# Four small marker loads between wq's second half and K in a one-core decode block

## The chip, the cores and the metric

The kernel runs on one core of a Trainium2 chip. The time is device microseconds of one execution; the kernel before took 137.87 us (median of three runs, 137.82 to 137.88). The profile is one further execution, and its times are counted from the start of its span.

## The reference

One decode step (one new token for each of 4 sequences) of an attention block and a gated MLP:

```
q   = layernorm(x) @ wq                       x: 4 x 1024, wq: 1024 x 4096
s   = q . K^T / sqrt(128)                     32 query heads, 4 KV heads, the last 2048 positions
o   = softmax(s) . V
h   = x + o @ wo                              wo: 4096 x 1024
n   = layernorm(h)
out = h + (silu(n @ w1) * (n @ w3)) @ w2      w1, w3: 1024 x 3584, w2: 3584 x 1024
```

All in bfloat16. With 4 rows of activations there is little arithmetic for each byte: the weights and the caches, 55.6 MB, are each read once.

## The kernel before

All big loads go through the sync queue (SP) into one buffer in SBUF, `ring`, of 160 KB in each partition. They are written out by hand in the list `plan`: wq's first half (4 of 8 blocks of rows), two "side" loads, wq's second half, K in four loads (two plan entries), V in four, wo, w1, w3 and w2 in four pieces of 17, 7, 3 and 1 rows. `load_next(n)` issues the next n entries. Seven are issued at the start (up to the first half of V), and the rest at fixed places in the program, once the ring's place is free: the second half of V after wq's first four blocks, wo after half of K, w1 after half of the V products, w3 in the wo product, and so on.

The side loads deserve a word. wq's second half leaves out the last 512 columns of its last block of rows (`load_tail`, line 126). Those come by `load_side` (line 120) as 20 and as 12 rows of four pieces of 1 KB, into tiles of the pool `ktpool`, and the q product takes them with eight matmuls of its own (line 273). `ktpool` has four buffers that are used in turn: the two side tiles take the first two, then the 16 transposed K tiles `kT` and four tiles `z` of the softmax follow.

Two small loads of x for the residual (`x_q`, line 169, 4 KB each) also go through SP, after the first seven entries. The first x (`x_sb`, line 158) and the output use the queue of ScalarE (ACT).

The framework gives each load on SP or ACT one of eight completion semaphores in turn. A load whose semaphore is still used by an earlier load makes its queue wait until that load has landed. So the position of a load in the program decides which earlier landing it waits for. In the kernel before, the fourth K load waits for wq's first half, the two first V loads for an x load and a side load, and the x_q loads for the other side load and for wq's second half.

The computation follows the loads: layernorm of x and the q product (line 263); for each of 16 pieces of K transposes on TensorE (line 319), copies by VectorE and ScalarE (lines 323 and 325) and scores (line 304); softmax; the V product (line 382); wo (line 411); the second layernorm; gate and up products (line 459); the down product (line 492), whose last 11 rows go to two accumulators that are cast to the result (lines 513 and 514) and stored.

Of the kernel before, what the change touches and what calls it, by code (L numbers as in the profile page):

```python
# [10 lines left out]
P = 128  # L11
# [3 lines left out]
BF16 = mybir.dt.bfloat16  # L15
# [4 lines left out]
def kernel(  # L20
# [13 lines left out]
    nc = tc.nc  # L34
# [23 lines left out]
    ktpool = ctx.enter_context(tc.tile_pool(name="ktpool", bufs=4))  # L58
# [6 lines left out]
    JG = 4  # L65
    QD = P // JG
# [56 lines left out]
    def load_tail(at, src, n, r0, m):  # L123
# [5 lines left out]
    plan = [  # L129
        ("wq", load_rows, (0, wq_v, N_Q, 0, 4)),  # L130
        ("side", load_side, SETS[0]),
        ("side", load_side, SETS[1]),
        ("wq", load_tail, (32 * KIB, wq_v, N_Q, 4, 4)),
        ("k", load_kv, (64 * KIB, A_k_cache, 0)),
        ("k", load_kv, (96 * KIB, A_k_cache, 2)),
        ("v", load_kv, (128 * KIB, A_v_cache, 0)),
        ("v", load_kv, (0, A_v_cache, 2)),
# [5 lines left out]
        ("w2", load_rows, (104 * KIB, w2_v, D, 24, 3)),  # L143
        ("w2", load_rows, (110 * KIB, w2_v, D, 27, 1)),
    ]
    loaded = {}
    cursor = [0]

    def load_next(n=1):
        for _ in range(n):  # L150
            if cursor[0] < len(plan):
                kind, f, args = plan[cursor[0]]
                loaded.setdefault(kind, []).extend(f(*args))
                cursor[0] += 1

    x_sb = act.tile([B, D], BF16)
    for c in range(2):
        nc.scalar.dma_start(out=x_sb[:, c * 512 : (c + 1) * 512], in_=x_flat[:, c * 512 : (c + 1) * 512])
    load_next(7)

    ident = const.tile([P, P], BF16)
    make_identity(nc, ident[:])
# [5 lines left out]
    for c in range(2):  # L168
        nc.sync.dma_start(
            out=x_q[c * 2 * QD : (c + 1) * 2 * QD : RS, :],  # L170
            in_=x_flat.rearrange("b (j c) -> j b c", j=JG)[2 * c : 2 * c + 2],
# [7 lines left out]
    for c in range(2):  # L179
# [8 lines left out]
        out=xn[:], in0=x_sb[:], scalar1=mv[:, 0:1], scalar2=rstd[:, 0:1],  # L188
# [14 lines left out]
    for r0, ne, ns in SETS:  # L203
# [3 lines left out]
            out=xs[:, len(sl) : len(sl) + ns, : ne * 4].rearrange("b l (i s) -> b l i s", s=4),  # L207
            in_=v[:, KC - 1, :, :, :],
        )
        for l in range(ns):  # L210
            nc.tensor.transpose(
                out=ts_ps[: ne * 4, len(sl), :], in_=xs[:, len(sl), : ne * 4], identity=ident[:B, :B]
# [4 lines left out]
    for _, ne, ns in SETS:  # L217
# [14 lines left out]
        out=perm[:].rearrange("p (h dq) -> p h dq", dq=JG),  # L232
        in_=ident[:].rearrange("p (dq h) -> p h dq", dq=JG),
# [12 lines left out]
    for j in range(2, JG):  # L246
        nc.vector.tensor_tensor(
            out=same[:, 0, :], in0=same[:, 0, :], in1=ident[:, j * QD : (j + 1) * QD], op=ALU.add
# [6 lines left out]
    for kc in range(KC):  # L255
        wq_t = loaded["wq"][kc]
        for hf in range(CQ // 512):
            for g in range(JG):
                c0 = g * CQ + hf * 512
                n = min(512, N_Q - CE - c0) if kc == KC - 1 else 512  # L260
# [23 lines left out]
    for r in range(REP):  # L284
        nc.tensor.transpose(out=qt_ps[:, r, :], in_=q_sb[:, r * Dh : (r + 1) * Dh], identity=ident[:])
    nc.vector.tensor_copy(
        out=qz[:, :, : Hkv * QD].rearrange("p b (g z) -> p b g z", g=Hkv)[:, :, :, :REP],
        in_=qt_ps[:].rearrange("p r (g x) -> p x g r", g=Hkv)[:, :B, :, :],
# [24 lines left out]
    for u, (b, n) in enumerate(units):  # L313
        k_v = loaded["k"][b]
        kT = ktpool.tile([P, NJ, P], BF16, tag="kT")
        for t in range(NJ // TB):
            kt_ps = psA.tile([P, TB, P], BF16, tag=f"kt{nt % 4}")
            for jj in range(TB):
                nc.tensor.transpose(  # L319
                    out=kt_ps[:, jj, :], in_=k_v[:, n * NJ + t * TB + jj, :], identity=ident[:]  # L320
# [21 lines left out]
        out=Pm[:], in_=scores_ps[:], func=ACT.Exp, bias=nmax[:], scale=1.0, accum_out=rsum[:]  # L342
# [6 lines left out]
    for c in range(NSB):  # L349
# [4 lines left out]
        for g in range(Hkv):  # L354
            if g % 2 == 0:
                nc.vector.tensor_scalar(  # L356
                    out=z[:, :, g, :], in0=pt_ps[:], scalar1=mask[:, g : g + 1], scalar2=None, op0=ALU.mult
# [10 lines left out]
        out=Dm[:], in0=ident[:].rearrange("p (g b r) -> p b g r", g=Hkv, b=B),  # L368
# [40 lines left out]
    for i in range(IO):  # L409
# [34 lines left out]
        out=hn[:], in0=h1[:], scalar1=tot[:, 0:1], scalar2=rstd2[:, 0:1],  # L444
# [5 lines left out]
        out=hnT[:].rearrange("p k x -> p (k x)"), in_=hn[:].rearrange("q (c k) -> q k c", k=KC)  # L450
# [3 lines left out]
    def gate_up(kind, out_ps):  # L454
# [27 lines left out]
        out=hgT[:].rearrange("p i x -> p (i x)"),  # L482
        in_=hg[:].rearrange("q s c -> q (s c)").rearrange("q (c i) -> q i c", i=IF),
# [62 lines left out]
```

## Time and profile before

| | |
|---|---|
| Time, median of 3 runs | 137.87 us (137.82 to 137.88) |
| Span of the profiled execution | 136.0 us; the page gives no total for that execution |
| Median less that span | 1.87 us |
| PE, DVE, ACT busy | 72.3, 43.9, 31.0 us |
| DMA packets, bytes, mean rate | 2650, 55.75 MB, 410 GB/s |
| of them on SP's queue | 2604 packets, 95.6% of the 16 DMA rings' time |
| wq's first half landed, second half landed | 12.9 us, 23.6 us |
| w1 issued | 76.27 us |
| last wait for a load on the chain | to 130.22 us |

The span goes from the first to the last instruction. "Busy" counts an engine's own instructions, not waiting. The DMA share is the mean busy share of the core's 16 DMA engines, called rings here: each load is cut over several of them, and each ring works its packets off in the order in which they were queued. Beside the page there is a record of every packet (queue, start, length, bytes); a completion is a packet of 4 bytes.

### The profile page before, as it was taken

To read this page: it belongs to the slowest core of one execution; us is meant where nothing else is said; L and a number is where in the kernel's file an instruction comes from. 1 tells how busy PE (TensorE), PEld (TensorE's weight loads), DVE (VectorE), ACT (ScalarE), POOL (GpSimd) and SP (SyncE) were. 2 spreads that over 40 slices of the span, in tenths; PEclk is the share of its full clock that TensorE was granted. 3 is DMA by queue.
4 is the path that set the end of the run, shared out by engine and by line. 5 is a ranking of instruction groups with operands and counts; after the bars stand their busy time and mean duration, and the time that the engine had idled before them with its cause. 6 is when DMAs were issued, how large, how long until landed. Compare 5 with 4: busy or idle time off the path is not lost.

```text
span 136.0 us, 2436 instructions
## 1 busy us (share of the span) xinstructions
PE 72.3 (53%) x1096; PEld 46.1 (34%) x1096; DVE 43.9 (32%) x79; ACT 31.0 (23%) x36; POOL 1.7 (1%) x8
## 2 busy tenths in 40 slices
PE   0004920979898989810525916791097000970981
PEld 0002300268374756500014905570043000430870
DVE  5055000043344444470994001206200596026010
ACT  3000000015555555609294300000001400000000
POOL 5000000000000000000000000000000000000000
PEclk9999975557999999985555555568556855568568
DMA  5999999999999999999989999989989899999970
GB/s 155 464 463 406 412 420 414 429 424 439 424 439 424 424 443 426 410 552 453 463 347 463 463 410 405 477 354 494 439 371 494 371 472 401 399 420 407 424 298 5
DMA packets 2650, 55.75 MB, mean 410 GB/s; under 512 B 296, under 2 KB 464, under 8 KB 720
## 3 DMA queue, kind: packets, MB, share of 16 engines
q1 hardware_dynamic: 2604, 55.58, 95.6%
q8 instruction: 8, 0.13, 0.3%
q10 hardware_dynamic: 36, 0.02, 0.0%
q14 instruction: 2, 0.02, 0.0%
HBM read 55.59 MB, written 0.01 MB: 409 GB/s over the span
## 4 chain that ended last, share of the span: by engine, by line
DMA 54%; PE 25%; ACT 11%; DVE 5%; SPq 2%; issue 1%; ACTq 0%
DMA ring<-in_B_w_dram 38%; DMA ring<-in_A_wq_dram 15%; PE kt_ps L319 11%; ACT kT L325 5%; PE scores_ps L304 5%; ACT z L360 3%; PE q_ps L263 3%; DVE rmax L336 2%; ACT Pm L341 2%; PE OT_ps L382 2%; DVE pT L350 1%; SPq L120 1%; PE g_ps L459 1%; DVE z L356 1%; ACT L341 1%
## 5 line engine op out<-in xcount | busy, mean ns | idle before, releaser
L325 ACT COPY kT<-kt_ps 128x1024 bf16<-128x1024 bf16 x16 | 15.9, 1013 | 13.4 <-PE kt_ps L319 13.4
L319 PE MATMUL kt_ps<-ident,ring 128*128 128x128 bf16 x256 | 18.0, 232 | 0.0
L319 PEld LDWEIGHTS <-ring 128*128 128x128 bf16 x256 | 16.0, 105 | 4.9 <-issue 4.9
L323 DVE COPY kT<-kt_ps 128x1024 bf16<-128x1024 bf16 x16 | 11.1, 692 | 16.5 <-PE kt_ps L319 16.5
L459 PEld LDWEIGHTS <-hnT 128*32 128x32 bf16 x128 | 5.5, 143 | 21.8 <-issue 19.2
L382 PE MATMUL OT_ps<-z,ring 128*128 128x32 bf16 x256 | 7.5, 188 | 8.5 <-ACT z L360 5.0
L459 PE MATMUL u_ps<-ring,hnT 128*32 128x448 bf16 x64 | 6.0, 563 | 11.0 <-DMA ring<-in_B_w_dram 11.0
L304 PE MATMUL scores_ps<-kT,qz 128*32 128x512 bf16 x64 | 9.9, 609 | 2.9 <-ACT kT L325 2.9
L263 PE MATMUL q_ps<-ring,xnT 128*4 128x512 bf16 x63 | 6.7, 595 | 7.8 <-DMA ring<-in_A_wq_dram 7.8
L382 PEld LDWEIGHTS <-ring 128*128 128x128 bf16 x256 | 7.4, 104 | 9.2 <-issue 9.2
L459 PE MATMUL g_ps<-ring,hnT 128*32 128x448 bf16 x64 | 5.9, 558 | 4.9 <-DMA ring<-in_B_w_dram 4.9
L492 PEld LDWEIGHTS <-hgT 128*32 128x32 bf16 x156 | 4.9, 134 | 6.2 <-issue 5.7
L411 PE MATMUL y_ps<-ring,o 128*32 128x256 bf16 x128 | 5.9, 371 | 0.8 <-DVE o L398 0.8
L514 ACT CAST res<-yb_ps 128x128 bf16<-128x128 f32 x1 | 0.3, 266 | 26.1 <-PE yb_ps L492 26.1
L492 PE MATMUL y_ps<-ring,hgT 128*32 128x256 bf16 x68 | 3.8, 419 | 4.4 <-DMA ring<-in_B_w_dram 4.4
L360 ACT ACTIVATE z<-pt_ps,mask 128x512 bf16<-128x512 f32 x8 | 5.3, 687 | 3.5 <-DVE z L356 3.5
L352 PE MATMUL pt_ps<-pT,perm 128*128 128x512 bf16 x4 | 2.4, 607 | 6.8 <-DVE pT L350 6.8
L263 PEld LDWEIGHTS <-xnT 128*4 128x4 bf16 x63 | 2.0, 115 | 11.7 <-issue 11.6
L194 PE MATMUL tp_ps<-ident,xn 4*128 4x4 bf16 x8 | 0.7, 200 | 10.0 <-DVE xn L187 10.0
L356 DVE TENSOR_SCALAR z<-pt_ps,mask 128x512 bf16<-128x512 f32 x8 | 5.5, 741 | 1.2 <-ACT z L360 0.8
L473 DVE RECIPROCAL eg<-eg 128x896 f32<-128x896 f32 x1 | 5.8, 5753 | 0.0
L411 PEld LDWEIGHTS <-o 128*32 128x32 bf16 x128 | 4.4, 131 | 3.1 <-DVE o L398 1.9
(85 smaller groups left out, 50.1 us busy)
## 6 DMA issues: line engine op xcount, KB each, us to landing
ring<-in_B_w_dram SPq DMA_DIRECT2D x2, 7168.0 KB, 22.5
ring<-in_A_k_cache_dram SPq DMA_DIRECT2D x4, 2048.0 KB, 27.6
ring<-in_A_v_cache_dram SPq DMA_DIRECT2D x4, 2048.0 KB, 29.2
ring<-in_B_w_dram SPq DMA_DIRECT2D x1, 4352.0 KB
ring<-in_A_wq_dram SPq DMA_DIRECT2D x1, 4096.0 KB, 12.2
ring<-in_A_wq_dram SPq DMA_DIRECT2D x1, 3968.0 KB
ring<-in_B_w_dram SPq DMA_DIRECT2D x1, 1792.0 KB
ring<-in_B_w_dram SPq DMA_DIRECT2D x1, 768.0 KB
```

What stands on the lines that cost most here:

```text
L263: nc.tensor.matmul(q_ps[QD * g : QD * g + B, hf * 512 : hf * 512 + n], lhsT=xnT[:, kc, :], rhs=wq_t[:, c0 : c0 + n], start=(kc == 0), stop ...
L304: nc.tensor.matmul(scores_ps[QD * g : QD * (g + 1), n * 512 : (n + 1) * 512], lhsT=qz_v[:, z0 : z0 + QD], rhs=kT_v[:, g, :, :], start=(b = ...
L319: nc.tensor.transpose(out=kt_ps[:, jj, :], in_=k_v[:, n * NJ + t * TB + jj, :], identity=ident[:])
L323: nc.vector.tensor_copy(out=kT[:, t * TB : (t + 1) * TB, :], in_=kt_ps[:])
L325: nc.scalar.copy(out=kT[:, t * TB : (t + 1) * TB, :], in_=kt_ps[:])
L356: nc.vector.tensor_scalar(out=z[:, :, g, :], in0=pt_ps[:], scalar1=mask[:, g : g + 1], scalar2=None, op0=ALU.mult)
L360: nc.scalar.mul(out=z[:, :, g, :], in_=pt_ps[:], mul=mask[:, g : g + 1])
L382: nc.tensor.matmul(OT_ps[:, b, :], lhsT=loaded["v"][b][:, j, :], rhs=PTz[j // NJ][:, (j % NJ) * B + b, :, :], start=(j == 0), stop=(j == J ...
L411: nc.tensor.matmul(y_ps[QD * j : QD * (j + 1), :], lhsT=o4[:, i, :, :].rearrange("p b s -> p (b s)"), rhs=loaded["wo"][i][:, j * CG : (j + ...
L459: nc.tensor.matmul(out_ps[QD * j : QD * (j + 1), hf, :HF], lhsT=hnT[:, k, :], rhs=loaded[kind][k][:, c0 : c0 + HF], start=(k == 0), stop=( ...
L473: nc.vector.reciprocal(out=eg[:], in_=eg[:])
L492: nc.tensor.matmul(out_ps[QD * j : QD * (j + 1), :n], lhsT=hgT[:, i, :], rhs=loaded["w2"][i][:, j * CG + c0 : j * CG + c0 + n], **kw,)
```

## The change

A new plan entry is put between wq's second half and the first K entry, so that eight entries are issued at the start. It takes one more tile of `ktpool` and loads into it four small rectangles of wo: 8 rows of 256 bytes, 10 of 320, 12 of 384 and 14 of 448, 16,128 bytes in all. Nothing reads the tile. No other operation is changed, but all later loads move on by four in the round of completion semaphores, and the `kT` tiles by one in the round of buffers: the fourth `kT` tile now follows the marks' tile.

```diff
+    MARKS = (8, 10, 12, 14)
+
+    def load_marks():
+
+        m = ktpool.tile([P, JG * QD * 16], BF16, tag="kT")
+        at = 0
+        for k in MARKS:
+            n = 16 * k
+            nc.sync.dma_start(out=m[:k, at : at + n], in_=A_wo[k * 128 : k * 128 + k, :n])
+            at += n
+        return []
+
+    plan.insert(4, ("marks", load_marks, ()))
...
-    load_next(7)
+    load_next(8)
```

## The prediction

> **What bounds the kernel now.** I read the page's slices first, then the stage table, the SP queue's own timeline with its list of waits, and the chain at the end.
>
> The page of the kernel before: span, DMA slices, and the SP queue's loads.
>
> ```profile
> span 136.0 us, 2436 instructions
> ...
> DMA  5999999999999999999989999989989899999970
> ...
> q1 hardware_dynamic: 2604, 55.58, 95.6%
> ```
>
> From the third slice almost to the end the 16 DMA rings are full, nearly all of it q1, the queue that SP fills. The stage table (columns: stage, its length, busy time of PE, PEld, DVE, ACT and POOL, granted clock, DMA share, GB/s) says the same:
>
> ```profile
> 3.00:12.90 9.90, 0.94 (x16) 0.90 (x17) 3.85 (x20) 0.29 (x1) 0.00 (x0) 1.00 0.97 417
> 12.90:21.40 8.50, 4.96 (x40) 1.57 (x40) 0.00 (x0) 0.00 (x0) 0.00 (x0) 0.85 1.00 430
> 21.40:23.70 2.30, 0.04 (x4) 0.04 (x7) 0.00 (x0) 0.00 (x0) 0.00 (x0) 0.50 0.98 419
> 23.70:36.00 12.30, 11.48 (x115) 7.14 (x114) 3.68 (x6) 3.81 (x5) 0.00 (x0) 0.64 1.00 428
> 36.00:60.00 24.00, 19.64 (x248) 12.71 (x244) 9.75 (x14) 12.68 (x13) 0.00 (x0) 1.00 1.01 430
> ```
>
> DMA share is 0.97 to 1.01, also where the chain of waits names PE and ACT (29 to 76 us): they use data that came earlier, while the rings load what is used later. I also followed the packet records of the trace ring by ring (each packet starts within about 16 ns of the end of the one before on its ring). No ring is idle from the first wq packet at 1.75 us to its last w2 packet. So the time is the number of nanoseconds that the fullest ring has to move, plus a tail.
>
> The SP queue (start, length, instruction; an entry of several holds the waits between them), and its waits up to 30 us (total, times, longest):
>
> ```profile
> 3.03 0.44 SPq L126 DMA_DIRECT2D ring<-in_A_wq_dram  x1
> 3.52 9.93 SPq L102 DMA_DIRECT2D ring<-in_A_k_cache_dram  x4
> 13.49 1.29 SPq L102 DMA_DIRECT2D ring<-in_A_v_cache_dram  x2
> 14.90 9.27 SPq L169 DMA_DIRECT2D x_q<-in_A_x_dram  x2
> ...
> SPq L169 <- DMA ring<-in_A_wq_dram: 8.2, 1, 8.2
> SPq L102 <- DMA ring<-in_A_wq_dram: 7.5, 1, 7.5
> ```
>
> SP runs far ahead of the rings. The fourth K load waits until wq's first half has landed at 12.9 us, because loads share eight completion semaphores in turn and one is reused only after its last load has landed. The x_q load waits in the same way for wq's second half.
>
> The end of the chain of waits (start, length, what):
>
> ```profile
> 100.48 29.74 DMA ring<-in_B_w_dram
> 130.22 0.04 issue
> 130.27 0.30 PE ya_ps L492 x3
> ...
> 132.46 0.17 PE ya_ps L492 x4
> ...
> 133.08 0.27 ACT res L514
> ```
>
> The seven-row piece of w2 lands at 130.22 and PE works without a pause to 133.06; the last piece lands at 132.68, just before PE needs it at about 132.74. Two of PE's limits, both DMA landings, lie within 0.1 us of each other.
>
> **The change, part by part.** The sum is made against the profiled execution: its span is 136.0 us; the median of the three runs is 137.87, so 1.87 us lie around the span, and I leave those as they are.
>
> *Bytes and packets on the rings (on the path).* A load is cut over a number of rings that divides its row count. The records show it: the first side load (20 rows, from source rows in groups of 5) puts 16 packets on each of 5 rings, the second (12 rows, groups of 3) 16 on each of 3, each x_q load 4 on each of 2; and these sets are nested, the two x_q rings among the three, the three among the five. So I take the marks to use 8, 10, 12 and 14 rings, one packet and one 4-byte completion on each, with the side loads' rings among them: 44 and 44 packets. Their price, from three rows of the records: two x_q loads follow each other on a ring in 100 ns each (4 packets of 512 B and a completion of 6 ns, so 23.5 ns a packet); 16 packets of 1024 B and a completion take 683 ns (42.3 each); a packet of 2048 B takes 80. That is a line of 4.7 ns plus 1 ns per 27.2 B. Packets of 256, 320, 384 and 448 B then cost 14, 16.5, 19 and 21 ns, 71 together, and four completions 24: 95 ns on a ring with all four marks, 75 with three, 52 with two, 27 with one, 0 on two rings. Nothing as small as 256 B is in the trace save completions. Bounds: as cheap as a completion each, 8 x 6 = 48 ns; as dear as a 1024 B packet, 4 x 42 + 24 = 193 ns. I take 95, by the line through the nearest rows.
>
> *Which ring is last.* At the end of the last w2 piece the 16 rings stand, in us, at 130.61, 130.85, 131.03, 131.23, 131.67, 131.89, 132.01, 132.15, 132.17, 132.21, 132.24, 132.25, 132.27, 132.27, 132.35 and 132.39 (the landings are about 0.3 later). The last one carries both side loads, so it is one of the nested three and gets all four marks; it is also the last at the seven-row piece. Both landings should therefore be 0.095 us later. If the marks went to other rings the last would stay, and the cost be 0 to 0.06: that is the lower bound.
>
> *The tail (on the path).* PE starts 0.095 us later at 130.32. Groups of four matmuls step at 0.107 us up to 131.6 and at 0.057 after, where the granted clock goes from 0.50 to 1.00 at 131.55. If that moment stays, about 0.05 of the delay remains for PE; but the last piece lands at 132.78 against PE's need at about 132.79. So the end moves by 0.05 to 0.1; I take 0.08. If the full clock came later with the work, the whole 0.1 would remain.
>
> *SP's issues and waits (beside the rings).* Four issues at 0.53 to 0.97 us each (x_q and side rows), 2.1 to 3.9 us of SP time. They also move every later load on by four places in the round of eight semaphores. Taking the turns in order, the third mark waits for an x load that landed early, the fourth for wq's first half at 12.9; so K's first load, until now issued at 3.52, goes out at about 13.5, then K's second and third behind the side loads (landed at 13.4 and 14.1), K's fourth at about 23.7 behind wq's second half (until now it waited for the first), then V and x_q. Who waits for that? The rings. The first ring to finish wq's second half does so at 21.40; the first load of all needed 1.02 us from its issue (0.73) to its first packet (1.75), so K must be issued by 20.4: 6.9 us to spare. K's fourth load is needed when the first ring ends the third, at 35.99: 11 us to spare. The third V load waits for K's first to land, and the wo load for PE, as before. Cost nothing; if the cover were gone, each us late would be a us on the end.
>
> *Buffers (beside).* The marks' tile takes a turn in the four kT buffers; the fourth kT tile's writers, a DVE and an ACT copy near 34 us, now also wait for four marks that landed some 10 us earlier. At 17 ns per extra semaphore instruction (SP's row) that is about 0.07 us for each engine, once. PE's stage has slack: w1 is issued at 76.27 after it, and its first packet can start only when a ring ends wo, at 79.73; less 1.02 that is 2.4 us of cover. Cost nothing.
>
> Sum: 137.87 + 0.08 = 137.95, with 48 to 193 ns for the marks if the last ring is hit.
>
> A rule that speaks against this: the Trainium skill, DMA: Bandwidth & Descriptors, section "Anatomy of one DMA", fits about 2.0 us of fixed cost to each DMA (for loads issued by GpSimd), and its "Rules for kernel authors" say that under 64 KB one pays mostly overhead. By that four marks in a row would be an estimated 8 us, 145.9; the x_q rows above, 4 KB a load and 0.1 us of a ring each, show that such latency isn't paid by a ring that has other work queued. The same page, "Why a DMA increments its semaphore by 16 and not by 1", states that on this path a load uses the lowest-numbered rings; the nested sets agree, and no row here shows ring numbers.
>
> **The rivals.**
> - *Hidden.* The marks lie on rings with room, or the tail absorbs them: 137.87, at most 137.92. For it: four rings end 1.2 us or more early. Against: the nested sets.
> - *Slower: lone packets stall their rings.* A one-packet load with its completion may not overlap its neighbours. The place is each ring between wq and K; the point from which it decides is 0.07 us of stall per mark (0.28 in all). At the longest, a whole 1.02 us start for each mark, it gives 137.87 + 4.1 = 142.0; at a tenth of that, 138.3. Against: completions between big loads leave no gap anywhere now.
> - *Slower: a fetch of instructions falls on another ring.* Eight packets of 16 KB on q8 now delay eight rings once each, by about 1.4 us with the neighbour that shares the ring, and none of them is a ring of the side loads. One on the last ring would give 139.3. The PE program isn't changed, which speaks against it.
> - *Slower: K late.* Needs SP held for 6.9 us more after 13.5; 2 us of it would give 139.9.
> - *Faster.* Twelve rings end within 0.7 us of the last, so no single ring's relief brings more than 0.04 us, and PE's tail is held by the last landing.
>
> **How the numbers follow.** About 0.2%, 0.28 us, is what a measurement of this kernel tells from no change. Forecast (0.05 to 0.2 us on the last ring) 0.50, hidden 0.27, stalls 0.10, a moved fetch 0.05, late K 0.03, faster for a reason not seen 0.05. Forecast and hidden lie within 0.2%: 0.77. Slower 0.18, faster 0.05. The range runs from 137.80, just under the runs before, to 138.25, which takes in twice the line's price and the mild end of the stalls.
>
> **What would show it.** Right: 88 more packets on q1, all under 512 B; K's issue moved from 3.5 to about 13.5 us; a DMA share still about 1.0 from 21 to 36 us; the seven-row piece landing about 0.1 us after 130.22. Wrong: a drop of the DMA share between 21 and 25 us (stall or late K), K's issue later than 20 us, or the last rings late by more than 0.3 us.

## The result

The changed kernel takes 138.63 us (median; 138.54 to 138.82) against 137.84 us (137.76 to 137.88) for the kernel before: a ratio of 1.0057, 95% interval 1.0044 to 1.0071. It is 0.79 us slower, where 0.08 had been forecast, and lies above the forecast's range.

The page of the changed kernel: its span, and the queue of SP's loads.

```profile
span 136.7 us, 2444 instructions
...
q1 hardware_dynamic: 2692, 55.60, 95.1%
```

The span grew by 0.74 us (136.741 less 135.999), nearly the whole loss. q1 has 88 packets more, 44 marks and 44 completions.

SP's queue in the changed kernel (start, length, instruction), and two rows of the stage table (stage, its length, busy time of PE, PEld, DVE, ACT, POOL, granted clock, DMA share, GB/s):

```profile
3.53 9.60 SPq L154 DMA_DIRECT2D m<-in_A_wo_dram  x4
13.17 11.08 SPq L102 DMA_DIRECT2D ring<-in_A_k_cache_dram  x4
24.30 1.26 SPq L102 DMA_DIRECT2D ring<-in_A_v_cache_dram  x2
```

```profile
21.40:23.70 2.30, 0.00 (x0) 0.00 (x0) 0.00 (x0) 0.00 (x0) 0.00 (x0) 1.00 0.95 398
23.70:36.00 12.30, 10.53 (x120) 5.60 (x119) 3.75 (x6) 4.55 (x5) 0.00 (x0) 1.00 1.01 430
```

K's loads are issued from 13.2 us in place of 3.5, as forecast, and the rings don't notice it: the DMA share is 0.95 where the marks pass (0.98 before; 1.02 in own_restore below, with the same marks) and 1.01 after. The packet records give the marks' price. On a ring with all four they start 20, 23 and 24 ns after each other, and 94 ns lie between the first of them and K's first packet; 95 had been worked out. The ring that is last ends its part of w2 at 132.52 us in place of 132.39. That is one profile against one. In the profiles below in which no instruction fetch has moved into the loads, the last w2 packet ends at 132.40 to 132.52 us in the four kernels with these marks and at 132.37 to 132.46 in the five without, 0.06 us apart in the mean.

So the rings account for about 0.13 us at the most. The rest is behind them. The end of the chain in the changed kernel (start, length, what):

```profile
101.53 31.28 DMA ring<-in_B_w_dram
132.81 0.04 issue
132.85 0.24 PE ya_ps L505 x4
133.09 0.08 PE yb_ps L505 x4
133.17 0.02 issue
133.20 0.27 ACT res L527
```

The last w2 piece lands at 132.81 (132.68 before) and ACT's cast of the result starts at 133.20 (133.08 before): 0.12 us late, no more. (In the same two groups of profiles the cast starts at 133.20 to 133.32 and at 133.08 to 133.16 us, 0.13 apart in the mean.) Then ACT's timeline at the end, first of the kernel before, then of the changed one:

```profile
133.08 0.27 ACT L514 CAST res<-yb_ps 128x128 bf16<-128x128 f32 x1 [26.10 <-PE yb_ps L492]
133.39 0.64 ACTq L515 DMA_DIRECT2D out_dram<-res  x1
```

```profile
133.20 0.27 ACT L527 CAST res<-yb_ps 128x128 bf16<-128x128 f32 x1 [26.64 <-PE yb_ps L505]
133.85 0.65 ACTq L528 DMA_DIRECT2D out_dram<-res  x1
```

Before, the output is issued 0.044 us after the cast's end (133.345 to 133.389); after, 0.385 us (133.463 to 133.848). Here 0.34 us are lost.

Last, SP's waits at the very end of the program (the last line of the kernel), the instruction group of the kernel before and of the changed one (count, then shortest, median and longest in ns, first and last start in us):

```profile
L541 SPq EVENT_SEMAPHORE  x7: 17/28/649, 125.9 to 135.9; - x7
```

```profile
L554 SPq EVENT_SEMAPHORE  x7: 17/28/28, 135.7 to 136.7; - x7
```

The program ends with five instructions on SP that wait for ten semaphores, two in each, in a fixed order: the eight completion semaphores and those that DVE and ACT raise. (The other two of the seven in the group come after them.) Before, the five start at 125.94, 130.24, 132.07, 132.70 and 135.18 us: four of them are over by the time that the output lands, at 135.16, since the output's semaphore is in the last. After, the output's semaphore is in the first: SP stands there until 135.67 and has the other four still to go, at 0.062 to 0.064 us each. From the output's landing to the end it is 1.092 us in place of 0.835.

| From the profiles of both, us | before | changed | difference |
|---|---|---|---|
| ACT's cast starts | 133.079 | 133.197 | +0.118 |
| cast's end to output's issue | 0.044 | 0.385 | +0.341 |
| issue to last landing | 1.775 | 1.801 | +0.026 |
| last landing to the end | 0.835 | 1.092 | +0.257 |
| end of the span | 135.999 | 136.741 | +0.742 |

### The profile page after: what moved, and what is told of

It is laid out like the page before. It is cut to its first block, busy times and chain, and to the rows that moved or that the text cites. A ratio compares the mean times of both kernels' runs of the same rounds, so it can differ in the third digit from the quotient of the medians.

```text
span 136.7 us, 2444 instructions
## 1 busy us (share of the span) xinstructions
PE 71.5 (52%) x1096; PEld 43.9 (32%) x1096; DVE 43.9 (32%) x79; ACT 30.9 (23%) x36; POOL 1.7 (1%) x8
## 4 chain that ended last, share of the span: by engine, by line
DMA 56%; PE 21%; ACT 13%; DVE 5%; SPq 2%; issue 1%; ACTq 0%
DMA ring<-in_B_w_dram 41%; DMA ring<-in_A_wq_dram 15%; PE kt_ps L332 9%; ACT kT L338 6%; PE scores_ps L317 5%; ACT z L373 3%; PE q_ps L276 3%; PE g_ps L472 2%; DVE rmax L349 2%; ACT Pm L354 2%; PE OT_ps L395 1%; DVE pT L363 1%; SPq L120 1%; DVE z L369 1%; ACT L354 1%
## 5 line engine op out<-in xcount | busy, mean ns | idle before, releaser
L332 PE MATMUL kt_ps<-ident,ring 128*128 128x128 bf16 x256 | 16.5, 219 | 0.0
L332 PEld LDWEIGHTS <-ring 128*128 128x128 bf16 x256 | 14.4, 98 | 5.0 <-issue 4.9
L472 PE MATMUL u_ps<-ring,hnT 128*32 128x448 bf16 x64 | 5.3, 516 | 11.6 <-DMA ring<-in_B_w_dram 11.6
L276 PE MATMUL q_ps<-ring,xnT 128*4 128x512 bf16 x63 | 7.2, 626 | 5.8 <-DMA ring<-in_A_wq_dram 5.8
L395 PEld LDWEIGHTS <-ring 128*128 128x128 bf16 x256 | 7.4, 105 | 8.6 <-issue 8.6
L472 PE MATMUL g_ps<-ring,hnT 128*32 128x448 bf16 x64 | 5.3, 510 | 6.6 <-DMA ring<-in_B_w_dram 6.6
L424 PE MATMUL y_ps<-ring,o 128*32 128x256 bf16 x128 | 6.4, 394 | 0.8 <-DVE o L411 0.8
L505 PEld LDWEIGHTS <-hgT 128*32 128x32 bf16 x156 | 4.4, 118 | 7.2 <-issue 6.5
L294 DVE TENSOR_SCALAR q_sb<-q_ps 128x512 bf16<-128x512 f32 x1 | 0.7, 692 | 14.9 <-PE q_ps L276 14.9
```

The lines of the kernel that those rows point to most:

```text
L276: nc.tensor.matmul(q_ps[QD * g : QD * g + B, hf * 512 : hf * 512 + n], lhsT=xnT[:, kc, :], rhs=wq_t[:, c0 : c0 + n], start=(kc == 0), stop ...
L332: nc.tensor.transpose(out=kt_ps[:, jj, :], in_=k_v[:, n * NJ + t * TB + jj, :], identity=ident[:])
L395: nc.tensor.matmul(OT_ps[:, b, :], lhsT=loaded["v"][b][:, j, :], rhs=PTz[j // NJ][:, (j % NJ) * B + b, :, :], start=(j == 0), stop=(j == J ...
L424: nc.tensor.matmul(y_ps[QD * j : QD * (j + 1), :], lhsT=o4[:, i, :, :].rearrange("p b s -> p (b s)"), rhs=loaded["wo"][i][:, j * CG : (j + ...
L472: nc.tensor.matmul(out_ps[QD * j : QD * (j + 1), hf, :HF], lhsT=hnT[:, k, :], rhs=loaded[kind][k][:, c0 : c0 + HF], start=(k == 0), stop=( ...
L505: nc.tensor.matmul(out_ps[QD * j : QD * (j + 1), :n], lhsT=hgT[:, i, :], rhs=loaded["w2"][i][:, j * CG + c0 : j * CG + c0 + n], **kw,)
```

## The experiments

The theory, named "semaphore turn" in the expectations: the ring cost is as forecast, and the rest comes from the four places by which all later loads move on in the round of eight semaphores. Against it "kT waits": the late issue on ACT comes from the two extra semaphore instructions with which ACT's copy for the fourth `kT` tile waits for the marks. And "rings alone": the marks' bytes are all of it.

| kernel | us | ratio to before, interval | cast to issue | landing to end |
|---|---|---|---|---|
| before | 137.84 | | 0.044 | 0.835 |
| changed | 138.63 | 1.0057 (1.0044 to 1.0071) | 0.385 | 1.092 |
| own_tile | 138.24 | 1.0030 (1.0018 to 1.0042) | 0.043 | 1.092 |
| restore | 138.53 | 1.0051 (1.0038 to 1.0064) | 0.394 | 0.836 |
| shift4 | 138.19 | 1.0029 (1.0018 to 1.0039) | 0.044 | 1.098 |
| own_restore | 138.00 | 1.0012 (1.0003 to 1.0020) | 0.044 | 0.835 |
| act1 | 137.81 | 1.0000 (0.9990 to 1.0010) | 0.043 | 0.840 |
| act2 | 138.16 | 1.0031 (1.0018 to 1.0044) | 0.392 | 0.835 |
| act3 | 138.32 | 1.0041 (1.0028 to 1.0054) | 0.044 | 0.840 |
| shift1 | 137.93 | 1.0011 (1.0001 to 1.0020) | 0.044 | 0.939 |
| marks_act1 | 138.65 | 1.0054 (1.0042 to 1.0067) | 0.045 | 1.087 |

The two columns at the right, in us, are from the profile of each. The ratios are to runs of the kernel before made beside each, with medians from 137.78 to 137.94 us.

**Marks in a tile of their own (own_tile).** `pad_t` is a tile of padding that nothing else uses.

```diff
-        pad_t = padpool.tile([P, pad_bytes], mybir.dt.uint8)
+        pad_t = padpool.tile([P, pad_bytes // 2], BF16)
...
-        m = ktpool.tile([P, JG * QD * 16], BF16, tag="kT")
+        m = pad_t
```

> The four marks stay where they are, but land in a tile of padding that nothing else uses, so the fourth kT tile's copies on DVE and ACT no longer wait for them (two semaphore instructions fewer on each). The round of completion semaphores is shifted by four as in the changed kernel. In the changed kernel 0.12 us of the loss stand at the last w2 landing, 0.34 us between the end of ACT's cast and the issue of the output (0.385 us against 0.044), and 0.25 us in SP's closing waits after the output has landed (five waits against one). Theory 'semaphore turn': all but the 0.12 comes from the shifted round, so this kernel is like the changed one: 138.6 us, output issued 0.38 us after the cast, closing waits as long. Rival 'kT waits': the extra semaphore instructions on ACT move its later instructions and delay the output's issue; then that gap falls to about 0.04 and the time to 138.3. Rival 'rings alone': the marks' bytes on the rings are all of it; then 138.6 too.

Measured: 138.24 us; the late issue is gone, the long closing is not. ACT's end in it:

```profile
133.32 0.27 ACT L527 CAST res<-yb_ps 128x128 bf16<-128x128 f32 x1 [26.01 <-PE yb_ps L505]
133.63 0.64 ACTq L528 DMA_DIRECT2D out_dram<-res  x1
```

So "kT waits" holds for the late issue. "Rings alone" falls: the rings carry the same marks.

**The round put right (restore).** On the changed kernel, with `pad_t` as above:

```diff
+    def load_tiny(at):
+
+        nc.sync.dma_start(out=pad_t[:8, at : at + 128], in_=A_wo[8:16, :128])
+        return []
+
+    plan += [("tiny", load_tiny, (1024 + i * 128,)) for i in range(4)]
...
-                load_next(3)
+                load_next(7)
```

> The changed kernel with four more tiny loads (8 rows of 256 bytes) on SP after the last piece of w2, which nothing reads and nobody waits for but the closing waits; they bring the output's completion semaphore back to the last in the closing order. Theory 'semaphore turn': closing waits fall back by 0.25 us, to 138.35; if the late issue of the output also goes with the semaphore, to 138.0. Rival 'kT waits': 138.35, the output's late issue (0.38 us) stays. Rival 'rings alone': 138.6, no change or a little more.

Measured: 138.53 us. The closing is back at 0.836 us, so its length goes with the output's place in the round. SP's closing waits in it, which begin again before the output lands:

```profile
L561 SPq EVENT_SEMAPHORE  x7: 17/28/28, 133.0 to 136.6; - x7
```

The late issue stays (0.394). The time fell by 0.1 us, less than the 0.26 us of the closing: in its profile the output took 1.95 us to land in place of 1.80, and why isn't shown. The tiny loads follow w2's last piece on the rings, and that piece's last landing comes 0.43 us after its last packet in place of 0.29.

**The round shifted without marks (shift4).** The same edit on the kernel before. ACT's copies are as they were, and nothing new is on the rings ahead of w2's last piece.

> The kernel before, without marks, and with the four tiny loads after the last piece of w2: the rings carry nothing new ahead of w2's last piece, and the output's semaphore moves by four, to the place that it has in the changed kernel. Theory 'semaphore turn': closing waits 0.25 us longer, 138.1 us; 138.45 if the late issue goes with the semaphore. Rival 'kT waits': 138.1, issue 0.04 us after the cast. Rival 'rings alone': 137.85.

Measured: 138.19 us, with the closing at 1.098 us and the issue at 0.044. Four loads that nobody reads, put behind all the others, cost 0.4 us (0.25 to 0.54 by the interval). Its profile shows 0.28 us, of which 0.26 are the closing waits. The first of them now starts when the output has landed:

```profile
L548 SPq EVENT_SEMAPHORE  x7: 17/28/28, 135.2 to 136.2; - x7
```

**Both put right (own_restore).** Marks in `pad_t` and the four tiny loads.

> Marks in the padding tile and the four tiny loads at the end: neither the kT copies nor the end of the round are changed, only the marks' 95 ns on the rings are left. Theory 'semaphore turn' and rival 'kT waits': 137.95, last landing of w2 about 0.1 us later than before, output issued 0.04 us after the cast, one closing wait after it lands. Rival 'rings alone': 138.6.

Measured: 138.00 us; both gaps are as before. The last w2 packet is 0.09 us later than before, near what was forecast for the marks, though such a difference lies within the spread of the profiles given above. The 0.22 us that are left (0.04 to 0.28 by the interval, which takes in the forecast's 0.08) hold that and probably what the tiny loads do to the last landing (0.39 us after the last packet in place of 0.29).

**Extra instructions on ACT (act1, act2, act3).** Is it the marks' semaphores, or only the number of instructions ahead of the output's issue? On the kernel before, with one, two and three of

```diff
+    for c in range(2):
+        nc.scalar.copy(out=pad_t[:, c * 16 : c * 16 + 16], in_=ident[:, :16])
```

which ACT does at 9.0 to 9.5 us, where it is otherwise idle.

> The kernel before with one more instruction on ACT, a copy of 128 x 16 elements into unused padding, done at about 6 to 10 us while ACT is idle; no marks, no shift of semaphores. In the two kernels whose kT copies wait for marks, ACT's output load was issued 0.385 to 0.394 us after the cast, in the four others 0.043 or 0.044 after it. Theory 'place in the stream': the two extra semaphore instructions push the output's issue past a point where ACT's sequencer must fetch its next instructions; then with one more instruction it is 0.04 or 0.39, whatever the kind of the instruction. Rival 'mark waits': it has to do with the waits on the marks' semaphores themselves; then 0.044 with any number of copies. Time 137.8 with 0.04, 138.15 with 0.39.

> As with one copy, but two: as many extra instructions ahead of the output's issue as the marks' waits brought. Theory 'place in the stream': the issue comes 0.39 us after the cast, 138.15 us, and the 8 KB packet on q14 starts right after the issue, near 134 us, in place of 135.65. Rival 'mark waits': 0.044 and 137.8.

> As with two copies, but three. Theory 'place in the stream': the fetch point lies one instruction earlier against the output's issue, so the fetch comes before or during the cast's wait; the issue is then at 0.04 again if the fetch is done ahead, or still late if it is not. Rival 'mark waits': 0.044 and 137.8.

Two copies make the late issue, one and three don't. ACT's end with two copies:

```profile
133.16 0.27 ACT L516 CAST res<-yb_ps 128x128 bf16<-128x128 f32 x1 [26.55 <-PE yb_ps L494]
133.82 0.64 ACTq L517 DMA_DIRECT2D out_dram<-res  x1
```

So it is the place in the instruction stream. The records of instructions say more. With one copy the gap stands one instruction later: ACT's closing drain starts 0.386 us after the end of the output's issue, where it is 0.040 in the kernel before and in the changed one, and there nobody waits. An 8 KB packet on the queue of instruction fetches (q14) starts at 135.65 us in the kernel before, at 135.24 with one copy, at 134.76 with two and at 108.78 with three. With three copies that fetch falls into the stream of loads:

```profile
q1 hardware_dynamic: 9, 0.52, 241.2%
q14 instruction: 1, 0.01, 3.9%
```

(the DMA queues of that kernel in the half microsecond from 108.7 us: packets, MB, share). Followed ring by ring, it falls on a ring that has also had one of the eight fetches of 16 KB on q8. It takes 0.31 us, and the packet after it 2.37 in place of 2.12, so that the ring loses 0.56 us; it ends at 132.72 us, and the next at 132.35. The three copies thus avoid the gap and lose 0.51 us all the same (0.39 to 0.74). What happens between the sequencer and its fetch isn't in the records: the late issue comes before the 8 KB packet, not after it. That both move together with the number of instructions is shown, the mechanism is not.

**One tiny load (shift1).** As shift4 with `range(1)` and `load_next(4)`.

> The kernel before with one tiny load after the last piece of w2: the output takes the next semaphore in the round, which SP's closing waits have in their third instruction. Theory 'semaphore turn': SP waits there for the output and then has two waits left at 0.062 to 0.064 us each, so that 0.96 us lie between the output's landing and the end (0.835 before, 1.092 to 1.098 with four); the time is 137.9. Rival: the closing cost comes with the number of extra loads on the queue, one fourth of 0.26: 0.90.

Measured: 137.93 us, 0.939 us from landing to end, which is 0.104 more than before: two instructions at 0.05. The group of SP's closing waits in it has one of 3.1 us, the one in which SP stands for the output, with two more to come:

```profile
L548 SPq EVENT_SEMAPHORE  x7: 17/28/3092, 126.0 to 136.0; - x7
```

0.96 had been expected by the place in the order and 0.90 by the number of loads; it lies between, nearer to the former, and the count of instructions that remain (two) is the one expected.

**Marks and one copy (marks_act1).** One copy on ACT, as above, in the changed kernel.

> The changed kernel with one copy of 128 x 16 elements on ACT into padding at 6 to 10 us, so that three instructions more than in the kernel before stand ahead of the output's issue. Theory 'place in the stream': as with three copies in the kernel before, the issue is 0.04 us after the cast, and the 8 KB fetch on q14 is near 109 us, where it costs its ring 0.3 us or more; the closing waits stay long. Time between 138.3 (fetch on a ring with room) and 138.7. Rival 'mark waits': issue 0.385 us after the cast still, 138.63.

Measured: 138.65 us, no better. The late issue is gone (0.045 us), and the fetch on q14 has moved to 108.99 us, onto a ring with all four marks and both side loads. That ring ends at 132.93 us, the next at 132.49, and the cast starts 0.52 us later than in the changed kernel. What was won at the issue was lost on the ring.

**Long marks (big_marks, big_spread, big_parts).** Does a byte on the fullest ring go to the end one for one? On own_restore:

```diff
-        m = pad_t
+        m = ring[:, 128 * KIB :]
...
-            n = 16 * k
-            nc.sync.dma_start(out=m[:k, at : at + n], in_=A_wo[k * 128 : k * 128 + k, :n])
+            n = 256 * k
+            nc.sync.dma_start(out=m[:k, at : at + n], in_=B_w1[k * 8 : k * 8 + k, :n])
```

> The kernel with marks outside kT and four tiny loads at the end (138.00 us, 0.22 over the kernel before), with rows sixteen times as long: 4096, 5120, 6144 and 7168 bytes, taken from w1 into the place that V has later. On a ring with all four that is 828 ns of bytes, 19 of packets and 24 of completions, 871 ns in place of 95. Theory 'fullest ring': bytes put on the ring that is last go to the end one for one, so 0.78 us more: 138.8 us, last w2 packet 0.78 us later. Rival 'spare ring time': K's part of the stream has room, and the time stays near 138.0; or the other rings' spread takes part of it, then between the two.

Measured: 143.43 us, ratio 1.0406 (1.0392 to 1.0421). Neither theory foresaw it: 5.4 us more than own_restore, for 0.26 MB. The stage in which the marks pass, with the short marks (own_restore) and with the long ones (columns as in the stage table above):

```profile
21.40:23.70 2.30, 0.01 (x2) 0.00 (x1) 0.00 (x0) 0.00 (x0) 0.00 (x0) 0.50 1.02 426
```

```profile
21.40:23.70 2.30, 0.00 (x0) 0.00 (x0) 0.00 (x0) 0.00 (x0) 0.00 (x0) 0.50 1.28 190
23.70:26.00 2.30, 0.00 (x0) 0.00 (x0) 0.00 (x0) 0.00 (x0) 0.00 (x0) 0.50 0.78 175
```

The rings are busy but move less than half: packets of 7168 bytes took up to 1.19 us (0.27 at the usual rate), and packets of wq and K beside them up to 3.55 and 2.37 us in place of 1.18 and 0.61. Two kernels ask why. First with the rows of each mark 448 KB apart in memory:

```diff
-in_=B_w1[k * 8 : k * 8 + k, :n]
+in_=B_w1[k : k + 64 * k : 64, :n]
```

> The kernel with the long marks (143.43 us, where 138.8 was expected: their packets took up to 1.19 us and packets of wq and K beside them up to 3.5 us) with one change: the rows of each mark are taken 64 rows of w1 apart (448 KB) in place of next to each other; sizes, rings and places in SBUF are the same. Theory 'one corner of memory': 8 to 14 rings that read neighbouring rows at once are served slowly, and so are their neighbours; then the packets of 7168 bytes fall to about 0.27 us and the time to 138.8 us. Rival 'same partitions': 14 rings that write partitions 0 to 13 at once hold each other up; then 143.4 again.

143.45 us, ratio 1.0402 (1.0385 to 1.0419): the distance of the sources is not it. Then with the first sources, and the rows going to every ninth partition:

```diff
-out=m[:k, at : at + n]
+out=m[: 9 * k : 9, at : at + n]
```

> The kernel with the long marks with one change: the rows of each mark go to partitions 0, 9, 18 and so on in place of 0, 1, 2; sources (neighbouring rows of w1), sizes and rings are the same. With sources 448 KB apart the time had stayed at 143.45 us. Theory 'same partitions': 14 rings that write partitions 0 to 13 at once hold each other up; here each ring writes into another group of eight or sixteen partitions, so the packets of 7168 bytes take about 0.27 us and the time is 138.8 us (0.78 over the kernel with the short marks). Rival: it is something else that the long one-packet loads do; then 143.4 again.

140.05 us, ratio 1.0164 (1.0145 to 1.0183), and 303 GB/s in the same stage:

```profile
21.40:23.70 2.30, 0.00 (x0) 0.00 (x0) 0.00 (x0) 0.00 (x0) 0.00 (x0) 0.50 1.06 303
```

Most of the excess, 3.4 of 5.4 us, goes with the partitions written: 0 to 13 by all rings at once, against every ninth one. The Trainium skill, SBUF — State Buffer, section "Door 1: The DMA port swizzle", states that DMA bandwidth depends on how many of 16 ports the partitions reach, and by its table partitions 0 to 13 reach four. The two kernels, which differ in the partitions alone, agree in direction. The remaining 2.05 us over own_restore are still 1.3 more than the bytes' 0.78; that stays open, and with it whether long loads on the fullest ring go one for one.

## Why the prediction was wrong

- **What bounds the kernel**: right. The rings stay full, and the last chain still begins at a w2 landing.
- **The marks' rings and their price**: right. 95 ns were worked out on a ring with all four marks, and 94 were measured; the sets of rings are nested as read from the side loads, since the rings with both side loads carry all four marks. The 2 us for each DMA that the Trainium skill fits for loads issued by GpSimd (DMA: Bandwidth & Descriptors, section "Anatomy of one DMA"), an estimated 8 us in all, were not paid by these loads from SP, which queue behind others.
- **The tail up to the cast**: the delay of 0.05 to 0.1 us, taken as 0.08, was measured as 0.118, and by a shorter path. In the changed kernel's profile the granted clock over the last stage was 0.98 (0.79 before); PE had caught up and waited for the last piece, so that landing alone (132.81 us for 132.68) sets the cast.
- **SP's issues and waits, "Cost nothing"**: this step failed first. The four places in the round of semaphores were read correctly, and I asked which loads would be issued late. To "Who waits for that?" I answered "The rings", and did not ask who else waits for these semaphores: the closing waits of SP, which stand in a fixed order and on the path. Before, the output's semaphore was the last of them; four places on, it was in the first. 0.257 us in the profile, shown by its coming with the shift alone (shift4) and going when the round is put right (restore, own_restore). The 1.87 us around the span, left as they were, are not at fault: they were 1.80 in the changed kernel's profiled run (138.54 less 136.74).
- **Buffers, "Cost nothing"**: this failed second. The extra semaphore instructions on ACT were seen (four were counted, and two came, each for two marks), priced at 17 ns each and set against PE's slack near 34 us. Their own time is indeed hidden. But they move all of ACT's later instructions by two places, and the output's issue, 100 us later, then comes 0.34 us late. Taking these waits away alone undoes it (own_tile), and two copies that have nothing to do with marks make it (act2).
- **The rivals**: the slower ones named (stalls of lone packets, a moved fetch, a late K) were not what happened. The moved fetch was near: in act3 and marks_act1 an instruction fetch does shift and costs its ring 0.56 us, but it was one on q14, and it moved with ACT's count of instructions.
- **The signs**: every sign named for "right" came: 88 small packets, K's issue at 13.2 us, a DMA share of 0.95 and 1.01 from 21 to 36 us, the seven-row piece at 130.34 us, 0.11 later. The time was outside the range all the same, for all of these signs lie ahead of the cast.
- **The chances**: 0.18 for slower was too little. All the mechanisms I had weighed lie ahead of the cast; the part behind it was assumed fixed.

## What to carry to other kernels

An extra load can cost more than its bytes: in a program like this it moves every later load on in the round of eight completion semaphores, and which one the last store gets decides how many closing waits come after it (about 0.06 us each here). Four loads moved the store from the last wait to the first, and four more moved it back. An extra instruction on the engine that issues the last store can cost 0.34 us or nothing, by its place in the instruction stream alone; a difference of a few tenths of a per cent between two kernels needs the last 3 us of both profiles compared before any theory of the stage that was edited. Where the bound is a full queue, price an addition in that queue, and then look separately at everything behind the last landing.

## What was not expected of the hardware

The output's issue is 0.04 or 0.39 us after the cast, with nothing between, for 0, 1, 2 and 3 extra instructions on ACT: 0.044, 0.043, 0.392, 0.044. The 8 KB instruction fetch on q14 can fall into the stream of loads (act3, marks_act1), and then holds one ring up by 0.56 us; that ring ended 0.37 and 0.44 us after the next one. And up to 14 rings that write 4 to 7 KB rows to partitions 0 to 13 at once brought the whole core's DMA from 426 to 190 and 175 GB/s for some 4.6 us, other loads included, while rows of 256 to 448 bytes to the same partitions cost a ring the 94 ns that small packets elsewhere led one to expect.
